# Shifting early work of a gated linear attention and squared-ReLU kernel from GpSimd to ScalarE and VectorE, with a new order of the whole program

## The chip, the cores and the metric

The kernel runs on 1 core of one Trainium2 chip. Times are device microseconds (us) of one launch. The time before is the median of three runs, 177.12 us (176.09, 177.12 and 177.60). One further run was profiled; its trace is what the text reads. Engines are named as in the profile: PE is TensorE, ACT is ScalarE, DVE is VectorE, POOL is GpSimd, SP is SyncE, which only issues transfers here.

## The reference

```python
# q, k, v, alpha: (4, 8, 768, 48) float32; w_in (384, 2048), w_out (2048, 384)
state = zeros((B, H, D, D))
for t in range(S):
    state = alpha[:, :, t, :, None] * state + einsum('bhd,bhe->bhde', k[:, :, t], v[:, :, t])
    y[:, :, t] = einsum('bhd,bhde->bhe', q[:, :, t], state)
x = y.transpose(0, 2, 1, 3).reshape(B * S, H * D)      # 3072 tokens x 384
h = maximum(x @ w_in, 0)
out = (h * h) @ w_out
```

A recurrence with a decay for each channel runs over 768 steps for each batch and head; its output, tokens by 384 features, goes through two matrix products with a squared ReLU between them.

## The kernel before

**Tiles.** The recurrence is computed in chunks of 128 tokens. Two chunks make a *pair* (256 tokens); 3 pairs make a batch element, and G = 12 pairs the whole, numbered g = 0 to 11. Every pair goes through the same stages:

- *loads* (L591): four transfers of 384 KB, in the order alpha, k, q, v, into the float32 buffer RAW (4 buffers).
- *decay* (L621; for pairs 0 and 1 in two halves X of four heads, decay_half, L664): ACT takes the logarithm of alpha (tile lab), PE sums it over the chunk with a triangular matrix, ACT takes exponentials (asb, and the decay over the whole chunk, acp), DVE multiplies q and k by them into bf16 (qks). In values (L612) v is cast to bf16 (vbf): on POOL for pairs 0 and 1 (L616), on ACT for the others (L619).
- *turned* (turned_half, L727, for pairs 0 and 1; turned, L701; turned_dma, L718, from pair 4 on): qks is transposed, by PE and an eviction into qkt, or by a transfer.
- *scores* (L759): PE multiplies k with q inside the chunk into four PSUM tiles of 128x512; DVE multiplies each by a triangular mask and writes bf16 (pm, L780).
- *carry* (L788): PE forms k^T v for each of the two chunks; DVE adds the old state (ust, L817) and POOL multiplies by the decay into the bf16 state (sbf, L819). The first chunk of a batch element has no old state: DVE makes it in one step (L814).
- *mixed* (L826; mixed_back, L897, from pair 4 on): PE sums pm times vbf (the 48 or 64 matmuls that need pm) and state times q (the matmuls of "before", two groups; the second must wait until the first has drained). For pairs 0 to 3 the result comes out transposed, and ACT evicts it chunk by chunk into xt, the transposed input of the MoE part (L879). For the others ACT evicts it into yb and a transfer transposes it into xt.
- *up* (L953): 8 steps u for each pair, 6 matmuls each: 256 hidden features, evicted by ACT with a ReLU (rr, 4 buffers, L973), squared by DVE (gt, L975). It needs both chunks of xt and the piece of win that holds its columns.
- *down* (L989): for each chunk tt four steps p of 4 matmuls each, from gt and wout into a PSUM tile, which ACT evicts and a transfer stores.

In the text "up/0/4" is step 4 of up for pair 0, "down/0/1/3" step 3 of chunk 1 of pair 0, "qks1" the tile qks of pair 1, and so on.

**Order.** Nobody writes the order by hand. Every operation is added to a Program with an engine, an assumed cost, a due time `at` and the tiles that it reads and writes; a list scheduler (Program.order, L147) then runs through assumed time and writes down one instruction list for each engine. At run time each engine executes its list strictly in order and waits by semaphores for what its next instruction needs. The due times come from TABLE (L16), one row for each pair, an offset for each stage. PSUM has eight banks: psG0 to psG3, psO0, psO1, psH0, psH1. POOLS (L30) says from which set the stages of pairs 0 and 1 take their bank; a bank is taken again only when its reader is done. The steps up use psH0 and psH1 in turn; WIDE (L37) counts the first steps that may also use psO0, which the steps down need. Where the scheduler finds PE idle early, it inserts matmuls on a tile of zeros ("warm", L982).

**Weights.** w_in and w_out come in nine pieces on POOL's queue, and the transfer casts them to bf16: win0, win2 (192 KB each), win4, win8, win12 (384 KB each), wout0, wout4, wout8, wout12 (384 KB each). PARTS (L38) makes two runs of them: the first six behind the landing of pair 1's alpha, then the last three. QUEUED (L40) puts the four loads of pair 2 on POOL's queue too, between the two runs. OPENS (L39) holds the loads of pair 3, on SP's queue, until wout8 has landed.

Of the kernel before, what the change touches and what calls it, by code (L numbers as in the profile page):

```python
# [5 lines left out]
ALU = mybir.AluOpType  # L6
AF = mybir.ActivationFunctionType
# [9 lines left out]
    dict(decay0=-101.63878, decay1=-64.79031, turned0=-73.57009, turned1=-62.54519, scores0=-30.02735, scores1=-46.13048, carry=-24.00248, mixed=-12.61483, up=3.82089, down=9.97184, scale00=37.96521, scale01=12.07767, scale10=-55.27694, scale11=66.26176, ends=3.96969, values=3.22532, loads=-198.59615),  # L17
    dict(decay0=-62.3532, decay1=-43.34947, turned0=-42.30728, turned1=-37.91382, scores0=-25.93696, scores1=-11.6373, carry=-24.1783, mixed=3.23949, up=7.51554, down=6.63429, scale00=34.30537, scale01=-58.35352, scale10=17.21724, scale11=40.27209, ends=44.67154, values=2.77668, loads=-199.72423),
    dict(decay=-3.52293, turned=6.45487, scores0=6.82966, scores1=6.65956, carry=-0.27539, mixed=10.50945, up=12.79282, down=3.90935, loads=-64.41188),
    dict(decay=7.24503, turned=8.97861, scores0=9.08238, scores1=9.71941, carry=9.32967, mixed=10.63684, up=15.57323, down=2.06012, loads=-61.40619),  # L20
    dict(decay=7.93117, turned=8.88166, scores0=11.15836, scores1=10.85679, carry=9.32967, mixed=11.76255, up=15.22484, down=2.29842, loads=-62.88919),
    dict(decay=8.06004, turned=10.03837, scores0=11.3686, scores1=10.90735, carry=10.59388, mixed=11.41181, up=16.11414, down=1.46618, loads=5.03271),
    dict(decay=7.68334, turned=10.80342, scores0=11.5973, scores1=11.84935, carry=10.99201, mixed=14.31953, up=16.37508, down=1.46618, loads=5.21441),
    dict(decay=11.20522, turned=12.7234, scores0=13.91124, scores1=13.85916, carry=12.42083, mixed=14.21671, up=16.27226, down=1.75528, loads=11.16392),
    dict(decay=11.49025, turned=11.82737, scores0=13.75226, scores1=14.7438, carry=12.85879, mixed=15.63875, up=17.67473, down=1.71467, loads=9.89433),
    dict(decay=11.5844, turned=11.68949, scores0=14.67671, scores1=14.63718, carry=14.26836, mixed=15.50289, up=17.56635, down=1.71467, loads=9.53939),
    dict(decay=10.86409, turned=12.68953, scores0=16.09372, scores1=14.63718, carry=14.3971, mixed=11.80752, up=17.60364, down=1.71467, loads=10.75129, masks=-31.23894),
    dict(decay=10.86409, turned=12.68953, scores0=15.58331, scores1=14.80708, carry=14.3971, mixed=15.0505, up=17.60364, down=1.71467, loads=10.84157),
# [8 lines left out]
WIDE = 0  # L37
PARTS = ((1, 3, 6), (2, -1, 3))  # L38
OPENS = {3: 7}  # L39
QUEUED = (2,)  # L40
# [385 lines left out]
def bass_gla_recurrent__then__act_relu_squared_kernel(  # L426
# [164 lines left out]
    def loads(g, at):  # L591
        b, t0, r = g // NW, (g % NW) * TW, g % NRAW
        for j, src in ((3, alpha), (0, k), (1, q), (2, v)):
# [5 lines left out]
            if g in QUEUED:  # L599
# [127 lines left out]
    def turned_half(g, X, at):  # L727
# [6 lines left out]
        for z in range(2):  # L734
# [17 lines left out]
            if X == 0:  # L752
                add("ACT", lambda act, dst=dst, src=src: act.activation(dst, src, AF.Copy), 480 * len(names) - 50,
                    at + 0.02 * z + 0.01, reads=[key], writes=[key] + names)
            else:
                add("DVE", lambda dve, dst=dst, src=src: dve.tensor_copy(dst, src), 280 * len(names) + 45,
                    at + 0.02 * z + 0.01, reads=[key], writes=[key] + names)

    def scores(g, at, js=range(NP), late=0.0):  # L759
# [19 lines left out]
        for n, ((i, X), (ps, key)) in enumerate(banks.items()):  # L779
            add("DVE", lambda dve, i=i, X=X, ps=ps: dve.tensor_tensor(  # L780
# [7 lines left out]
    def carry(g, at, spots=None):  # L788
# [17 lines left out]
        for c in chunks:  # L806
# [9 lines left out]
            else:  # L816
                add("DVE", lambda dve, u=u, was=was, pv=pv: dve.tensor_tensor(UST[u][:], pv, was, ALU.add),  # L817
                    270, at + 0.05 * c, reads=[key, ("sbf", old)], writes=[key, ("ust", u)])
                add("POOL", lambda e, u=u, to=to, ac=ac: e.tensor_tensor(to, UST[u][:], ac, ALU.mult),  # L819
                    600, at + 0.05 * c, reads=[("ust", u), ("acp", c_, 0), ("acp", c_, 1)], writes=[("sbf", new)], port=True)  # L820
# [5 lines left out]
    def mixed(g, at, spots=None, between=None):  # L826
# [50 lines left out]
        for c in range(2):  # L877
            ps, key = banks[c]
            add("ACT", lambda act, c=c, ps=ps: act.activation(  # L879
                XT[:, 2 * (g % NX) + c].rearrange("f k (p i) -> f k i p", i=2),  # L880
                ps[:, 0:HD].rearrange("f (k i p) -> f k i p", k=KT, i=2), AF.Copy),
                    435, at + 0.02 * c + 0.01, reads=[key], writes=[key, ("xt", g % NX, c)])
# [145 lines left out]
    def stage(at, fn, *name):  # L1028
        place[name] = at
        stages.append((at, fn, name))  # L1030
# [3 lines left out]
    for g in range(G):  # L1034
        o = TABLE[g]
        stage(2 * g + o["loads"], lambda at, g=g: loads(g, at), "loads", g)
# [69 lines left out]
    for run, (r, j, n) in enumerate(PARTS):  # L1106
        first = pieces[sum(p[2] for p in PARTS[:run])][0]
        ahead(("weights", run), [("weights", run + 1), ("up", 0) if first == "in" else ("down", 0)])
        ahead(("loads", r), [("weights", run)])
    for g in QUEUED:  # L1110
        ahead(("weights", g - 2), [("loads", g)])
# [64 lines left out]
```

## Time and profile before

| what | us |
|---|---|
| median of three runs | 177.12 |
| the runs | 176.09 to 177.60 |
| the profiled execution, own time | 177.66 |
| its span, first to last instruction | 175.9 |
| PE busy in the span | 168.3 |
| DVE busy | 120.3 |
| ACT busy | 116.8 |
| POOL busy | 38.5 |

The granted PE clock is full throughout. The profiled execution's own time is 1.76 us longer than its span. A row of the timeline reads: start in us, busy us, engine, line, operation, written tile <- read tile, shape, count, and in brackets the idle time of the engine just before and what ended it. "psG<-vbf,qks" on PE is carry, "psG<-pm,vbf" and "psG<-qkt,sbf" are mixed, "psG<-qkt" is scores, "psG<-lab,hinc" decay, "<-ident,qks" the transposes, "psH<-xt,win" up and "psO<-wout,gt" down.

### The profile page before, as it was taken

The numbers are of one execution on the slowest core, as the hardware profiler recorded it, in microseconds if no ns is written. First come the engines' busy times: TensorE is split into PE (matmuls) and PEld (weight loads), VectorE is DVE, ScalarE is ACT, GpSimd is POOL, SyncE is SP. The second block draws the span as 40 slices with busy tenths as digits, with TensorE's granted clock in tenths as the row PEclk, the third lists the DMA queues.
The fourth block names the chain that finished last, engine by engine and source line by source line (L and its number), as shares of the span: only waits on it lengthen the run. The fifth ranks groups of instructions, "written<-read, shape, count | busy, mean of one in ns | idle before, by whom it ended". The sixth has DMA issues, their size and how long they took to land.

```text
span 175.9 us, 5997 instructions
## 1 busy us (share of the span) xinstructions
PE 168.3 (96%) x2609; PEld 123.8 (70%) x2609; DVE 120.3 (68%) x253; ACT 116.8 (66%) x233; POOL 38.5 (22%) x68
## 2 busy tenths in 40 slices
PE   7899598999999999999999999999999999999994
PEld 7556466766778677786777777776777777777773
DVE  7887844986899899888737939877885551232220
ACT  3884458666889677489868697767675545656641
POOL 4099820100012001010222131212330302220120
PEclk9999999999999999999999999999999999999999
DMA  5999999899996994999999989999491133212222
GB/s 146 324 294 173 203 338 221 140 276 246 318 321 100 307 304 101 148 315 201 324 201 319 238 159 296 195 321 173 100 182 32 22 71 60 56 22 48 45 45 91
DMA packets 76314, 32.89 MB, mean 187 GB/s; under 512 B 69632, under 2 KB 75456, under 8 KB 76288
## 3 DMA queue, kind: packets, MB, share of 16 engines
q1 hardware_dynamic: 70384, 25.04, 61.4%
q0 software_dynamic: 5904, 7.47, 20.7%
q8 instruction: 20, 0.33, 0.8%
q14 instruction: 6, 0.05, 0.1%
HBM read 25.17 MB, written 4.72 MB: 170 GB/s over the span
## 4 chain that ended last, share of the span: by engine, by line
PE 85%; DMA 9%; POOL 2%; ACT 1%; DVE 1%; issue 1%
PE psO L996 34%; PE psH L963 33%; DMA win<-in_moe_w_in_dram 6%; DMA xt<-yb 3%; PE psG L770 3%; PE psO L982 2%; PE psG L920 2%; POOL win L574 2%; PE psG L799 2%; PE psG L838 2%; PE psO L1015 2%; PE psG L910 1%; PE psG L710 1%; PE psG L637 1%; DVE qks L691 1%; ACT asb L688 1%
## 5 line engine op out<-in xcount | busy, mean ns | idle before, releaser
L973 ACT ACTIVATE rr<-psH 128x512 bf16<-128x512 f32 x96 | 58.2, 611 | 37.6 <-PE psH L963 36.5
L963 PE MATMUL psH<-xt,win 128*128 128x256 bf16 x576 | 75.8, 273 | 2.5 <-DMA win<-in_moe_w_in_dram 2.1
L996 PE MATMUL psO<-wout,gt 128*128 128x384 bf16 x368 | 71.5, 326 | 0.7 <-ACT xt L879 0.7
L975 DVE TENSOR_TENSOR gt<-rr 128x512 bf16<-128x512 bf16 x96 | 41.4, 439 | 38.4 <-ACT rr L973 37.9
L963 PEld LDWEIGHTS psH<-xt,win 128*128 128x128 bf16 x576 | 54.0, 98 | 16.1 <-ACT rr L973 3.1
L996 PEld LDWEIGHTS psO<-wout,gt 128*128 128x128 bf16 x368 | 35.0, 98 | 17.3 <-ACT xt L879 0.9
L949 POOL DMA_DIRECT2D out_dram<-osb x28 | 15.1, 544 | 71.3 <-ACT osb L1003 71.0
L780 DVE TENSOR_TENSOR pm<-psG,mask 128x512 bf16<-128x512 f32 x45 | 28.7, 682 | 1.8 <-PE psG L770 0.6
L819 POOL TENSOR_TENSOR sbf<-ust,acp 128x192 bf16<-128x192 f32 x16 | 9.3, 580 | 52.4 <-DVE ust L817 52.3
L658 DVE TENSOR_TENSOR qks<-raw,asb 128x768 bf16<-128x768 f32 x20 | 18.3, 951 | 3.2 <-ACT asb L647 3.2
L1003 ACT ACTIVATE osb<-psO 128x384 f32<-128x384 f32 x23 | 11.4, 494 | 3.7 <-PE psO L996 3.2
L647 ACT ACTIVATE asb<-psG 128x384 bf16<-128x384 f32 x20 | 9.8, 492 | 2.9 <-PE psG L639 2.6
L627 DVE TENSOR_TENSOR raw<-raw 128x384 f32<-128x384 f32 x20 | 11.0, 564 | 0.1
L770 PEld LDWEIGHTS psG<-qkt 64*64 64x64 bf16 x360 | 6.0, 106 | 4.3 <-issue 2.7
L770 PE MATMUL psG<-qkt 64*64 64x128 bf16 x360 | 8.7, 220 | 0.1
L619 ACT ACTIVATE vbf<-raw 128x768 bf16<-128x768 f32 x10 | 8.5, 853 | 0.2 <-DMA raw<-in_v_dram 0.2
L936 ACT ACTIVATE yb<-psG 128x384 bf16<-128x384 f32 x14 | 6.4, 490 | 2.5 <-PE psG L910 1.8
L982 PE MATMUL psO<-warm 128*128 128x128 bf16 (+1 forms) x39 | 7.0, 343 | 1.1 <-DVE warm L518 1.1
L817 DVE TENSOR_TENSOR ust<-psG,sbf 128x192 f32<-128x192 f32 x15 | 5.3, 353 | 2.5 <-PE psG L799 1.4
L627 DVE TENSOR_TENSOR raw<-raw,ro 128x384 f32<-128x384 f32 x10 | 6.1, 612 | 0.2 <-DMA raw<-in_q_dram 0.2
L643 ACT ACTIVATE ro<-raw 128x384 f32<-128x384 f32 x10 | 5.2, 518 | 0.4 <-DMA raw<-in_alpha_dram 0.4
L633 ACT ACTIVATE lab<-raw 128x384 bf16<-128x384 f32 x10 | 5.2, 524 | 0.2 <-DVE raw L627 0.2
(98 smaller groups left out, 131.0 us busy)
## 6 DMA issues: line engine op xcount, KB each, us to landing
raw<-in_alpha_dram SPq DMA_DIRECT2D x11, 384.0 KB, 4.7
raw<-in_k_dram SPq DMA_DIRECT2D x11, 384.0 KB, 4.8
raw<-in_q_dram SPq DMA_DIRECT2D x11, 384.0 KB, 4.8
raw<-in_v_dram SPq DMA_DIRECT2D x11, 384.0 KB, 5.6
out_dram<-osb POOLq DMA_DIRECT2D x28, 96.0 KB, 3.3
out_dram<-osb SPq DMA_DIRECT2D x9, 192.0 KB, 4.3
wout<-in_moe_w_out_dram POOLq DMA_DIRECT2D x4, 384.0 KB, 14.3
win<-in_moe_w_in_dram POOLq DMA_DIRECT2D x3, 384.0 KB, 9.5
```

The lines of the kernel that those rows point to most:

```text
L627: add("DVE", lambda e: e.tensor_tensor(dst, a0, a1, ALU.mult), 470, at_, reads=reads, writes=writes, port=True)
L647: add("ACT", lambda act, z=z: act.activation(ASB[a][:, z, 0, :], ps[:, 0:HD], AF.Exp, scale=2.0 * z - 1.0), 372, at + 0.04 + 0.02 * z, rea ...
L658: add("DVE", lambda dve, z=z, decays=decays: dve.tensor_tensor(QKS[x][:, z, :, :, 0:D], both(r, z), decays, ALU.mult), 870, at + 0.05 + 0. ...
L770: last = pe.matmul(banks[i, j // 2][0][64 * c:64 * c + 64, col:col + 128].rearrange("p (a b) -> p a b", a=2), QKT[t][64 * i:64 * i + 64, 0 ...
L780: add("DVE", lambda dve, i=i, X=X, ps=ps: dve.tensor_tensor(PMB[m][:, i, 2 * X:2 * X + 2].rearrange("p j n s -> p j (n s)"), ps[:].rearran ...
L949: add(by, lambda e, dst=dst, ps=ps: e.dma_start(dst, OSB[o][ps, :]), 600, at + 0.01 * i, reads=[("osb", o)], dma=("own" if by == "POOL" el ...
L963: last = pe.matmul(ps[:, f * TW:(f + 1) * TW].rearrange("p (c t) -> p c t", c=2), WIN[:, kt, fj * 128:(fj + 1) * 128], XT[:, 2 * (g % NX): ...
L973: add("ACT", lambda act: act.activation(ro, ri, AF.Relu), 480, at, reads=[key], writes=[key, ("rr", r)])
L975: add("DVE", lambda dve: dve.tensor_tensor(gt[:, 2 * u:2 * u + 2, :], rr, rr, ALU.mult), 340, at, reads=[("rr", r)], writes=[("gt", g % NG ...
L982: last = pe.matmul(psO[1][:, 0:128 * wide].rearrange("p (a b) -> p a b", a=wide), WARM[:], bass.AP(tensor=WARM, offset=0, ap=[[128, 128], ...
L996: last = pe.matmul(ps[:, 0:DM], GT[g % NGT][:, fj, tt * 128:(tt + 1) * 128], WOUT[:, fj, :], start=(fj == 0), stop=(fj == FT - 1))
L1003: add("ACT", lambda act: act.activation(OSB[o][:], ps[:, 0:DM], AF.Copy), 372, at, reads=[key], writes=[key, ("osb", o)])
```

## The change

For pairs 0 and 1 four kinds of operation change their engine, by new constants:

- CASTS: the cast of v goes from POOL to ACT (the code of the other pairs, L619).
- STATES: the three products ust times decay (the second chunk of pair 0, both of pair 1) go from POOL to DVE.
- XTS: the second of the two evictions of xt goes from ACT to DVE.
- COPIED: one of the four mask products of each pair is made in two steps: ACT copies the PSUM tile into an rr buffer in bf16, and DVE multiplies that by the mask. That is tile 1 (second score bank of the first half) for pair 0 and tile 2 for pair 1.
- TURNS: the eviction of the second transposed half of pair 1 goes from DVE to ACT.

Beside that the whole order is new: all numbers of TABLE, POOLS and WEIGHTS, and WIDE is 10 instead of 0, so that all steps up of pair 0 and the first two of pair 1 rotate over psH0, psH1 and psO0, and the first step down comes behind them. The loads of pairs 0 and 1 get due times of their own for alpha, for k and q, and for v.

What the two built programs show, engine by engine:

- SP issues the loads of pairs 0 and 1 in the same order as before. Further on, pair 5's loads stand ahead of the first two stores of output instead of behind the first.
- POOL: the two casts and three of the state products are gone; the nine pieces of weights and the loads of pair 2 stand in the same order as before.
- PE has the same work (96 steps up, 100 down, 33 groups of mixed, 22 of scores, 14 of decay, 12 of transposes, 11 of carry) and the same count of changes between matmul forms behind down/0/1/3. In the first 40 us its order differs, as follows.

PE before, from the second decay on: scores/0 (first half), transposes of pair 1's first half, carry/0, mixed/0 (48), transposes of the second half between the two groups of mixed/0, scores/1 (first), up/0/0, up/0/1, scores/1 (second), up/0/2 to up/0/6, carry/1, mixed/1 (48), up/0/7, down/0/1/0, the two groups of mixed/1, down/0/0/0, up/1/0, and so on.

PE after: scores/0 (both halves, ahead of pair 1's decay), transposes of the first half, mixed/0 (48), transposes of the second half, carry/0, first group of mixed/0, carry/1, second group of mixed/0, scores/1 (first), up/0/1, up/0/0, scores/1 (second), up/0/2, up/0/3, mixed/1 (48) and its first group, up/0/4, its second group, up/0/5, up/0/6, up/0/7, up/1/0 to up/1/3, down/0/0/0, up/1/4, up/1/5, decay/2, down/0/1/0, up/1/6, up/1/7, down/0/0/1, carry/2, transposes of pair 2, down/0/0/2, down/0/1/1, down/0/1/2, scores/2, down/0/0/3, down/0/1/3.

```diff
 TABLE = [
-    dict(decay0=-101.63878, decay1=-64.79031, turned0=-73.57009, turned1=-62.54519, scores0=-30.02735, scores1=-46.13048, carry=-24.00248, mixed=-12.61483, up=3.82089, ...
+    dict(decay0=-97.00571, decay1=-78.81219, turned0=-80.03886, turned1=-50.01967, scores0=-30.48193, scores1=-47.68772, carry=-27.42287, mixed=-10.34508, up=13.54943, ...
...
-POOLS = [dict(decay=0, turned=2, scores=2, carry=1, mixed=2), dict(decay=2, turned=2, scores=1, carry=0, mixed=1)]
-WEIGHTS = (-75.69063, -62.43345)
+POOLS = [dict(decay=1, turned=2, scores=2, carry=1, mixed=2), dict(decay=0, turned=1, scores=1, carry=1, mixed=0)]
+WEIGHTS = (-75.27555, -73.28278)
...
-WIDE = 0
+WIDE = 10
...
-QUEUED = (2,)
+QUEUED = ((2, None, 'loads', 0),)
+CASTS = ('ACT', 'ACT')
+STATES = ('DVE', 'DVE')
+XTS = ('DVE', 'DVE')
+COPIED = ((1,), (2,))
+TURNS = ('DVE', 'ACT')
...
     def values(g, at):
...
-        if g < FIRST:
+        if g < FIRST and CASTS[g] == "POOL":
...
     def turned_half(g, X, at):
...
-            if X == 0:
+            if X == 0 or TURNS[g] == "ACT":
...
     def scores(g, at, js=range(NP), late=0.0):
...
+            if g < FIRST and 2 * X + i in COPIED[g]:
+                r = copied[0] % NRR
+                copied[0] += 1
+                add("ACT", lambda act, ps=ps, r=r: act.activation(RR[r][:], ps[:], AF.Copy), 480, at + late + 0.01 * n,
+                    reads=[key], writes=[key, ("rr", r)])
+                add("DVE", lambda dve, i=i, X=X, r=r: dve.tensor_tensor(
+                    PMB[m][:, i, 2 * X:2 * X + 2].rearrange("p j n s -> p j (n s)"),
+                    RR[r][:].rearrange("p (j s) -> p j s", j=2), mask, ALU.mult),
+                    340, at + late + 0.01 * n, reads=[("rr", r), "mask"], writes=[("pm", m, i, X)], port=True)
+                continue
...
     def carry(g, at, spots=None):
...
-                add("POOL", lambda e, u=u, to=to, ac=ac: e.tensor_tensor(to, UST[u][:], ac, ALU.mult),
-                    600, at + 0.05 * c, reads=[("ust", u), ("acp", c_, 0), ("acp", c_, 1)], writes=[("sbf", new)], port=True)
+                by = STATES[g] if g < FIRST else "POOL"
+                add(by, lambda e, u=u, to=to, ac=ac: e.tensor_tensor(to, UST[u][:], ac, ALU.mult),
+                    600 if by == "POOL" else 270, at + 0.05 * c, reads=[("ust", u), ("acp", c_, 0), ("acp", c_, 1)], writes=[("sbf", new)], port=True)
...
     def mixed(g, at, spots=None, between=None):
...
+            if g < FIRST and c == 1 and XTS[g] == "DVE":
+                add("DVE", lambda dve, dst=dst, src=src: dve.tensor_copy(dst, src), 470, at + 0.02 * c + 0.01,
+                    reads=[key], writes=[key, ("xt", g % NX, c)])
+                continue
```

More of the change, by code (lines that the diff above doesn't have):

```diff
@@ L1108, in bass_gla_recurrent__then__act_relu_squared_kernel @@
         ahead(("weights", run), [("weights", run + 1), ("up", 0) if first == "in" else ("down", 0)])
[L1109 to L1111 removed]
+        if r >= FIRST:
+            ahead(("loads", r), [("weights", run)])
+    for g in range(FIRST):
+        ahead(("loads", g), [("pair", g)])
+        ahead(("pair", g), [("last", g)])
+        ahead(("last", g), [("decay", g)])
+        for run, (r, j, n) in enumerate(PARTS):
+            if r == g and j >= 0:
+                ahead((("pair", g) if j < 2 else ("last", g) if j == 2 else ("loads", g)), [("weights", run)])
+    for g, j, name, run in QUEUED:
+        ahead(("weights", run), [(name, g)])
+        if run + 1 < len(PARTS):
+            ahead((name, g), [("weights", run + 1)])
     for g, x in OPENS.items():
```

45 lines of the change are left out of this document (25 added, 20 removed).

## The prediction

> **What bounds the kernel now.** First the page's parts 1 and 2: which engine fills the span, and where it does not.
>
> ```profile
> span 175.9 us, 5997 instructions
> PE 168.3 (96%) x2609; PEld 123.8 (70%) x2609; DVE 120.3 (68%) x253; ACT 116.8 (66%) x233; POOL 38.5 (22%) x68
> PE   7899598999999999999999999999999999999994
> PEclk9999999999999999999999999999999999999999
> ```
>
> PE is the bound at full clock. Its only thin slices are the first six (4.4 us each, to 26 us) and the last one. The windows view gives the same by stage (PE first, DMA share second to last):
>
> ```profile
> 20.00:24.00 4.00, 2.26 (x22) 1.66 (x26) 2.54 (x4) 1.68 (x3) 1.32 (x2) 1.00 1.22 272
> 28.00:32.00 4.00, 3.96 (x39) 3.08 (x40) 1.99 (x5) 4.00 (x11) 0.00 (x0) 1.00 1.30 202
> 40.00:50.00 10.00, 10.00 (x192) 7.33 (x190) 7.62 (x15) 7.22 (x16) 0.00 (x0) 1.00 1.06 289
> ```
>
> From 28 us on PE has no gap to speak of, so whatever the change does to DVE, ACT or POOL there is worth nothing unless PE has to wait. A gain can only come from the head: useful matmuls done before 28 us that now run later. What PE waited for, from the waits of PE:
>
> ```profile
> PE psH L963 <- DMA win<-in_moe_w_in_dram: 2.1, 3, 1.5
> PE psO L996 <- ACT xt L879: 0.7, 1, 0.7
> ```
>
> That is 2.8 us, 2.1 for pieces of win and 0.7 for the xt of pair 1. PE's timeline shows where:
>
> ```profile
> 12.45 0.44 PE L799 MATMUL psG<-vbf,qks 64*64 64x48 bf16 x32
> 16.29 1.48 PE L963 MATMUL psH<-xt,win 128*128 128x256 bf16 x12
> 21.40 1.47 PE L963 MATMUL psH<-xt,win 128*128 128x256 bf16 x12 [1.55 <-DMA win<-in_moe_w_in_dram]
> 23.21 0.82 PE L963 MATMUL psH<-xt,win 128*128 128x256 bf16 x6 [0.34 <-DMA win<-in_moe_w_in_dram]
> 25.00 0.83 PE L963 MATMUL psH<-xt,win 128*128 128x256 bf16 x6
> 25.67 0.81 PE L996 MATMUL psO<-wout,gt 128*128 128x384 bf16 x4
> 27.92 0.82 PE L996 MATMUL psO<-wout,gt 128*128 128x384 bf16 x4 [0.71 <-ACT xt L879]
> 28.58 0.82 PE L963 MATMUL psH<-xt,win 128*128 128x256 bf16 x6
> 37.63 2.76 PE L996 MATMUL psO<-wout,gt 128*128 128x384 bf16 x16
> 40.32 0.86 PE L838 MATMUL psG<-pm,vbf 64*64 64x128 bf16 x48
> ```
>
> At 21.40 PE stood 1.55 us for win8 while carry and mixed of pair 1 were still to do: they ran at 24 to 27 us, behind the steps up that wait for weights. Why they were not ready is in POOL's timeline:
>
> ```profile
> 8.36 0.82 POOL L616 CAST vbf<-raw 128x768 bf16<-128x768 f32 x1 [4.80 <-DVE qks L691]
> 9.34 4.01 POOL L574 DMA_DIRECT2D win<-in_moe_w_in_dram  x5 [0.16 <-issue]
> 19.85 0.90 POOL L616 CAST vbf<-raw 128x768 bf16<-128x768 f32 x1
> 24.97 0.61 POOL L819 TENSOR_TENSOR sbf<-ust,acp 128x192 bf16<-128x192 f32 x1 [3.56 <-DVE ust L817]
> 26.05 0.51 POOL L819 TENSOR_TENSOR sbf<-ust,acp 128x192 bf16<-128x192 f32 x1 [0.47 <-DVE ust L817]
> ```
>
> The cast of pair 1's v stood on POOL behind all issues of weights and of pair 2 (19.85); carry/1 needs it; then two state products on POOL, ending 25.58 and 26.56, stand before the last groups of mixed/1.
>
> **The change, part by part.** The anchor is the state "up/0/7, mixed/1 and xt of pair 1 done, up/1/0 about to start". Before, that is 28.58 with two steps down (0.65 each) done too. I follow the changed order to the same state. Rows of ACT and of DVE:
>
> ```profile
> 9.07 0.94 ACT L670 ACTIVATE lab<-raw 128x384 bf16<-128x384 f32 x2 [0.35 <-DMA raw<-in_alpha_dram]
> 10.19 1.92 ACT L688 ACTIVATE asb<-psG 128x384 bf16<-128x384 f32 x4 [0.18 <-PE psG L676]
> 12.56 1.02 ACT L753 ACTIVATE qkt<-psG 128x1024 bf16<-128x1024 bf16 x1 [0.25 <-PE psG L742]
> 14.23 0.61 ACT L879 ACTIVATE xt<-psH 128x384 bf16<-128x384 f32 x1 [0.65 <-PE psH L838]
> 31.75 0.86 ACT L619 ACTIVATE vbf<-raw 128x768 bf16<-128x768 f32 x1
> 35.19 1.25 ACT L973 ACTIVATE rr<-psH 128x512 bf16<-128x512 f32 x2 [1.60 <-PE psH L963]
> 10.94 1.12 DVE L691 TENSOR_TENSOR qks<-raw,asb 128x384 bf16<-128x384 f32 x2
> 13.65 0.35 DVE L814 TENSOR_TENSOR sbf<-psG,acp 128x192 bf16<-128x192 f32 x1
> 17.02 0.68 DVE L780 TENSOR_TENSOR pm<-psO,mask 128x512 bf16<-128x512 f32 x1
> 17.79 0.42 DVE L975 TENSOR_TENSOR gt<-rr 128x512 bf16<-128x512 bf16 x1
> ```
>
> *Casts of v.* On ACT a cast is 0.86 us (31.75). Pair 0's stands between the evictions of qkt (done about 8.6) and pair 1's logarithm, which therefore starts at 9.35 instead of 9.07: 0.3 us on the path. On POOL the issue of weights no longer waits for a cast, only for pair 1's alpha (9.07): 0.27 us earlier at most, and 0 at least, since the transfers share engines that are already full (DMA share 1.22 at 20 to 24 us). I take 0.1 for the landings.
>
> *Mask in two steps.* ACT pays 0.6 (a copy of 128x512, half of 1.25), DVE 0.42 instead of 0.68. Pair 0's copy stands on ACT between the logarithms and the exponentials of pair 1, so these run 10.7 to 12.65 instead of 10.19 to 12.11: with the cast 0.5 us later.
>
> *State products on DVE.* 0.35 each (the nearest row, L814, has the same shape) instead of 0.61 and 0.51, and no hand-over between engines. If DVE takes longer from SBUF than from PSUM, POOL's 0.61 is the high end. Nothing excludes less: from 192 to 512 elements a product grows from 0.35 to 0.68, 1 ns an element, so 0.2 without any fixed part is the low end. I take 0.35, the row of the same shape.
>
> *Second xt eviction on DVE.* No row; between 0.35 (192 elements) and 0.68 (512), so 0.53 for 384, against 0.61 on ACT. The ends, 0.18 us either way, go into the range. The second transposed half of pair 1 costs ACT 1.02 more.
>
> *The chain.* ACT: exponentials to 12.65; first transposed half of pair 1 at 13.25 (qks ready 12.75, and 0.5 as before: 12.06 to 12.56) to 14.3; first xt of pair 0 14.2 to 14.8, as before (14.23); cast of v1 14.65 to 15.5; second transposed half 15.4 to 16.4. DVE: third mask 10.94 to 11.6, two qks to 12.75, bf16 mask to 13.1, two qks to 14.05. PE: mixed/0 (48) 13.15 to 14.0, the transposes to 14.4, carry/0 14.45 (before 12.45); DVE makes the three state steps 15.0 to 15.9; carry/1 waits for the cast, 15.55 to 16.0; second group of mixed/0 to 16.35; DVE's xt 16.4 to 16.95; the first step up at 17.0. **That is 0.7 us later than before (16.29); so far the change loses.**
>
> Then steps up at 0.655 each (1.31 for two: 28.58 and its followers): up/0/1 and up/0/0 to 18.35, scores/1 (second) to 18.7, up/0/2 and up/0/3 to 20.1. Meanwhile DVE does masks and states; its list ends with the bf16 mask at 20.25. mixed/1 (48) 20.3 to 21.1, its first group to 21.4, **in the time in which PE stood for win8**; up/0/4 21.45 to 22.1 (win8 landed before 21.4), second group to 22.4, up/0/5 to 23.1, up/0/6 behind win12 (23.2 before, 23.1 now) to 23.8, up/0/7 to 24.5. DVE's xt of pair 1 is done at 23.05, so up/1/0 follows at once: the anchor state at 24.5, without the two steps down.
>
> From there to the end of down/0/1/3 PE needed 40.24 - 28.58 = 11.66 us before (37.63 and 2.6 us of 16 matmuls); with the two steps down, 1.30, it is 12.96, so 37.46 now. **Gain 40.24 - 37.46 = 2.78 us.** As a check: the waits of the head that go are 2.1 + 0.7 = 2.8. Behind that point both orders hold the same matmuls and as many changes of form, so the rest takes 175.9 - 40.24 us in both, if PE does not wait.
>
> Does it? PE now reaches the weights sooner. Landings, from the transfers by window (us from issue to landing) and SP's own queue:
>
> ```profile
> raw<-in_v_dram SPq DMA_DIRECT2D x1, 384.0 KB, 4.9
> win<-in_moe_w_in_dram POOLq DMA_DIRECT2D x1, 384.0 KB, 10.5
> wout<-in_moe_w_out_dram POOLq DMA_DIRECT2D x1, 384.0 KB, 13.7
> 33.28 0.37 SPq L604 DMA_DIRECT2D raw<-in_alpha_dram  x1
> ```
>
> The v of pair 1, issued at 7.79, landed at 12.7, 2 us before its cast. The last piece of win landed at 23.1; wout4, issued at 17.63, at 31.3; wout8 just before 33.28. Behind 24.5 come eight steps up, two down and decay/2 (0.25), so the changed order asks for wout4 at 24.5 + 5.2 + 1.3 + 0.3 = 31.3, and for wout8 behind carry/2 and the transposes of pair 2 at about 33.3: no slack, no wait. ACT was busy for all 4.00 us at 28 to 32 us with PE at 3.96: nearly a second bound, now in the same stretch. I cost both at nothing; what hides them is just enough, and without that cover up to 1 us comes back, the high end. The first step down now needs psO0 free from up/1/1, which is evicted a step before; that costs nothing while ACT keeps up. On SP, pair 5's loads pass two stores; a store that waits holds nobody, as there are eight buffers for the output. Later, before had one wait of PE on a transfer in all:
>
> ```profile
> 134.84 0.82 PE L963 MATMUL psH<-xt,win 128*128 128x256 bf16 x6 [0.25 <-DMA xt<-yb]
> ```
>
> There mixed/8 ended 8 us of PE work ahead of the step up that needs it or the next; counted by the same durations along the new list of PE, pairs 7 to 11 have 10 to 15 us, so 0.25 more can go, and pairs 4 to 6 have about as much room as before.
>
> *The pages.* The Trainium skill, "SBUF — State Buffer", section "Who interferes with whom", says that a VectorE instruction with two SBUF inputs contends with a GpSimd instruction that reads SBUF. The trace agrees:
>
> ```profile
> 19.38 2.31 DVE L975 TENSOR_TENSOR gt<-rr 128x512 bf16<-128x512 bf16 x3
> ```
>
> Three squares took 0.77 each in place of 0.42 while POOL cast v (19.85); by that rule about 1 us of DVE time comes back in the head. It is off PE's path there, so my sum does not use it.
>
> **The rivals.**
>
> *A. As above.* Span 175.9 - 2.78 = 173.1, own time 174.9. The profiled execution (177.66) lies 0.54 above the median shown, so against the median 177.12 - 2.75 = 174.4. Own range: 173.3 (the wait at 134.84 gone, weights 0.27 earlier, states at 0.2) to 175.3 (1 us lost at wout4, wout8 or ACT).
>
> *B. PE runs into transfers that it outran.* The order is ahead of the data: 31.3 asked against 31.3 landed, and pair 3's loads still start only when wout8 has landed (33.28). Each 0.5 us that a landing slips is a wait at wout4, wout8 or at pair 3's transposes, and up to 2 us of the gain go. For it speaks the DMA share of 1.2 to 1.3; against it, that PE has steps of pair 1 to do in between. Time 177.1 - 1.1 = 176.0.
>
> *C. Slower: the cast on ACT in front of carry/1.* PE is in order: carry/1 stands ahead of the second group of mixed/0, and so of every step up. If v1's cast ends late (v1 landing later because weights start earlier, or ACT's queue of 8 to 15 us slipping), all steps up slip with it. To cancel the gain the cast must end 2.8 us later, at 18.3 instead of 15.5; that needs v1 to land at 17.4 rather than 12.7, or ACT, DVE and PE handing over 0.2 us slower at each of some 14 steps from 9 to 17 us. With 4.5 us of delay the time is 177.1 + 1.7 = 178.8. The slack of 2 us on v1 speaks against it; that every step of this stretch is a hand-over speaks for it.
>
> *D. Nothing changes:* the time of the head is set by win12's landing at 23.1 whatever stands before it, and the work taken out of the gap comes back as waits for ACT. Time 177.1 - 0.1 = 177.0.
>
> **How the numbers follow.** A 0.62, B 0.20, C 0.12, D 0.06. The predicted time is A's, 174.4. The range goes from A's low end, 173.3, through B and D to 177.1, leaving out C and little else. About 1%, 1.8 us (175.3 to 178.9), is what a measurement of this kernel can tell from no change. Faster by over 1%: A and a fifth of B, 0.66. Within: the rest of B, D and some of C, 0.24. Slower: 0.10.
>
> **What would show it.** Right: in the changed trace the first step up starts later than 16.29, near 17.0; mixed/1 of PE stands at 20 to 22 us; no wait of over 0.5 us for win; up/1/0 starts near 24.5; down/0/1/3 ends near 37.5; POOL computes nothing between 4 and 30 us. Wrong: up/1/0 later than 26 (C), or PE waits of over 1 us in all between 25 and 60 us on transfers of wout, raw or on ACT (B), or a wait for the transposes behind 60 us.

## The result and the profile after

The changed kernel takes **174.18 us** (median of six runs, 173.92 to 175.52), the kernel before in the same rounds 177.03 (176.09 to 177.60). The ratio is 0.9859, with a 95% interval of 0.9817 to 0.9902. Forecast were 174.4 us and a range of 173.3 to 177.1. The profiled execution took 174.21 us, its span is 172.5.

The page's parts 1 and 2 of the changed kernel:

```profile
span 172.5 us, 6016 instructions
PE 167.6 (97%) x2611; PEld 123.9 (72%) x2611; DVE 119.4 (69%) x257; ACT 116.9 (68%) x236; POOL 36.4 (21%) x63
PE   7889999999999999999999999999999999999994
```

The thin slices of PE behind the third have gone. The waits of PE:

```profile
PE psO L1004 <- DVE warm L523: 1.1, 1, 1.1
PE psH L747 <- DVE qks L696: 0.4, 1, 0.4
PE psG L856 <- issue: 0.3, 1, 0.3
PE psG L747 <- DVE qks L696: 0.3, 1, 0.3
```

Neither win nor xt is in the list any more; what is left lies before 21 us. PE's timeline:

```profile
14.36 0.44 PE L816 MATMUL psG<-vbf,qks 64*64 64x48 bf16 x32
16.74 0.83 PE L985 MATMUL psH<-xt,win 128*128 128x256 bf16 x6
20.02 0.64 PE L856 MATMUL psG<-pm,vbf 64*64 64x128 bf16 x32
20.98 0.42 PE L856 MATMUL psG<-pm,vbf 64*64 64x128 bf16 x16 [0.32 <-issue]
21.50 0.83 PE L985 MATMUL psH<-xt,win 128*128 128x256 bf16 x6
23.88 1.47 PE L985 MATMUL psH<-xt,win 128*128 128x256 bf16 x12
31.34 0.81 PE L1018 MATMUL psO<-wout,gt 128*128 128x384 bf16 x4
35.97 2.88 PE L1018 MATMUL psO<-wout,gt 128*128 128x384 bf16 x16
```

The reader is to see mixed/1 at 20.02, where before PE stood for win8. The row at 23.88 holds up/0/7 and up/1/0, so up/1/0 starts at about 24.54 with no gap. The last row holds four steps, of which down/0/1/3 is the second: it ends near 37.4, and before that was 40.24. At 20.98 a pause of PE in the midst of mixed/1 ends, for which the profile names no wait ("issue"). From its start to up/0/4 mixed/1 takes 1.48 us here, 0.96 in a run without a pause that is shown below, so the pause costs about 0.5. A few rows of ACT, of DVE and of POOL:

```profile
14.48 0.83 ACT L624 ACTIVATE vbf<-raw 128x768 bf16<-128x768 f32 x1
```
```profile
15.65 0.36 DVE L837 TENSOR_TENSOR sbf<-ust,acp 128x192 bf16<-128x192 f32 x1
16.09 0.59 DVE L900 CAST xt<-psH 128x384 bf16<-128x384 f32 x1
19.55 0.41 DVE L792 TENSOR_TENSOR pm<-rr,mask 128x512 bf16<-128x512 bf16 x1
19.89 1.66 DVE L997 TENSOR_TENSOR gt<-rr 128x512 bf16<-128x512 bf16 x4
```
```profile
9.50 4.00 POOL L579 DMA_DIRECT2D win<-in_moe_w_in_dram  x5 [5.95 <-DMA raw<-in_alpha_dram]
```

v1's cast ends at 15.31, and nothing stands on POOL between the issues. The last mask of pair 1 ends at 19.96, 0.06 us before mixed/1 starts: DVE's list now sets that start.

### The profile page after: what moved, and what is told of

It is laid out like the page before. It is cut to its first block, busy times and chain, and to the rows that moved or that the text cites. A ratio compares the mean times of both kernels' runs of the same rounds, so it can differ in the third digit from the quotient of the medians.

```text
span 172.5 us, 6016 instructions
## 1 busy us (share of the span) xinstructions
PE 167.6 (97%) x2611; PEld 123.9 (72%) x2611; DVE 119.4 (69%) x257; ACT 116.9 (68%) x236; POOL 36.4 (21%) x63
## 4 chain that ended last, share of the span: by engine, by line
PE 95%; DVE 2%; issue 1%; ACT 0%
PE psH L985 36%; PE psO L1018 36%; PE psG L777 4%; PE psO L1004 3%; PE psG L856 2%; PE psG L942 2%; PE psG L816 2%; PE psO L1037 2%; PE psG L932 2%; PE psO L985 2%; DVE qks L696 2%; PE psG L642 1%; PE psG L715 1%; PE psG L681 1%; PE psH L856 1%
## 5 line engine op out<-in xcount | busy, mean ns | idle before, releaser
L995 ACT ACTIVATE rr<-psH 128x512 bf16<-128x512 f32 x92 | 55.3, 612 | 22.6 <-PE psH L985 20.6
L985 PE MATMUL psH<-xt,win 128*128 128x256 bf16 x552 | 70.5, 273 | 0.0
L1018 PE MATMUL psO<-wout,gt 128*128 128x384 bf16 x368 | 70.0, 326 | 0.0
L985 PEld LDWEIGHTS psH<-xt,win 128*128 128x128 bf16 x552 | 52.7, 98 | 11.6 <-DVE xt L900 0.2
L997 DVE TENSOR_TENSOR gt<-rr 128x512 bf16<-128x512 bf16 x96 | 40.3, 434 | 29.6 <-ACT rr L995 29.3
L1018 PEld LDWEIGHTS psO<-wout,gt 128*128 128x128 bf16 x368 | 34.3, 98 | 17.8 <-ACT osb L1025 0.3
L797 DVE TENSOR_TENSOR pm<-psG,mask 128x512 bf16<-128x512 f32 x44 | 27.9, 682 | 3.7 <-PE psG L777 2.9
L624 ACT ACTIVATE vbf<-raw 128x768 bf16<-128x768 f32 x12 | 10.1, 842 | 0.0
L632 DVE TENSOR_TENSOR raw<-raw,ro 128x384 f32<-128x384 f32 x10 | 5.5, 551 | 0.8 <-DMA raw<-in_q_dram 0.5
L654 ACT ACTIVATE ro<-ro 128x384 f32<-128x384 f32 x10 | 5.2, 524 | 0.1
```

The lines of the kernel that those rows point to most:

```text
L624: add("ACT", lambda act: act.activation(dst, src, AF.Copy), 740, at, reads=raw(r, 2), writes=[("vbf", vb)])
L632: add("DVE", lambda e: e.tensor_tensor(dst, a0, a1, ALU.mult), 470, at_, reads=reads, writes=writes, port=True)
L797: add("DVE", lambda dve, i=i, X=X, ps=ps: dve.tensor_tensor(PMB[m][:, i, 2 * X:2 * X + 2].rearrange("p j n s -> p j (n s)"), ps[:].rearran ...
L985: last = pe.matmul(ps[:, f * TW:(f + 1) * TW].rearrange("p (c t) -> p c t", c=2), WIN[:, kt, fj * 128:(fj + 1) * 128], XT[:, 2 * (g % NX): ...
L995: add("ACT", lambda act: act.activation(ro, ri, AF.Relu), 480, at, reads=[key], writes=[key, ("rr", r)])
L997: add("DVE", lambda dve: dve.tensor_tensor(gt[:, 2 * u:2 * u + 2, :], rr, rr, ALU.mult), 340, at, reads=[("rr", r)], writes=[("gt", g % NG ...
```

## The experiments

In seven kernels the changed kernel's own order was kept: its finished lists were taken and single operations were moved from one engine's list to another's, nothing else. "Row of up/0/7" is the start of the PE row that is at 23.88 in the changed kernel; both columns of rows are from the one profiled execution of each kernel. The ratio is to the kernel before on the same chip.

| kernel | median us (runs) | ratio, 95% interval | first step up | row of up/0/7 |
|---|---|---|---|---|
| changed | 174.18 (6) | 0.9859, 0.9817 to 0.9902 | 16.74 | 23.88 |
| casts on POOL, v1's behind the issues | 181.90 (4) | 1.0290, 1.0258 to 1.0321 | 22.93 | |
| casts on POOL, v1's between the issues | 174.28 (4) | 0.9868, 0.9840 to 0.9895 | 17.26 | 23.88 |
| states on POOL, between the issues | 174.62 (4) | 0.9866, 0.9833 to 0.9898 | 16.67 | 23.65 |
| second xt on ACT | 174.64 (4) | 0.9891, 0.9864 to 0.9918 | 17.05 | 24.19 |
| masks in one step | 174.44 (4) | 0.9879, 0.9853 to 0.9905 | 16.78 | 23.75 |
| transposed half on DVE | 174.32 (4) | 0.9873, 0.9838 to 0.9909 | 16.82 | 23.52 |
| all five moves undone | 175.06 (5) | 0.9914, 0.9891 to 0.9936 | 17.93 | 25.14 |
| moves with the old numbers | 176.85 (10) | 1.0022, 0.9995 to 1.0049 | 18.89 | |
| two copies before v1's cast | 175.60 (10) | 0.9939, 0.9902 to 0.9977 | 19.06 | 27.11 |
| four copies before v1's cast | 178.44 (10) | 1.0049, 1.0007 to 1.0090 | 19.53 | 26.16 |
| weights issued 1 us later | 175.66 (10) | 0.9926, 0.9892 to 0.9960 | 16.69 | 23.92 |

One thing has to be known for reading the last column. Ten of these kernels have the changed kernel's list on PE. Of their profiles only one, that with the second xt on ACT, has a pause in mixed/1 as long as the changed kernel's (20.28 to 21.82, 1.54 us up to up/0/4); the others need 0.96 to 1.10 us there, for 1.48. So up to 0.5 us of any delay ahead of mixed/1 is made up at this place, and a row of up/0/7 that is no later does not show by itself that a move costs nothing. How many of the executions that were not profiled have the pause is not known.

**The place of the casts.** Theory: what held carry/1 and mixed/1 back was the place of v1's cast behind all issues on POOL. Rival D: the landing of win12 sets the head, whatever stands before it. Two kernels put both casts back on POOL; `move` takes an operation to another engine's list, behind a named one or at its planned time.

```diff
+    issue = [o for o in pr.programs["POOL"] if o.dma is not None][:13]
+    pr.move(kept["cast", 0][0], "POOL", [o for o in pr.programs["POOL"] if o.start < issue[0].start][-1], ...)
+    pr.move(kept["cast", 1][0], "POOL", issue[-1], ...)
```

> The changed kernel with both casts of v back on POOL at the places they had before: pair 0's ahead of the weights, pair 1's behind all issues of weights and of pair 2's loads; every other list is kept as it is. Theory (the gain is pair 1's carry and mixed done before win8, and the cast's place in POOL's queue kept them from it): the cast ends at about 21.0 instead of 15.3, carry/1 and with it every step up slips by 5.5 us; PE regains some of it since it is ahead of the weights by 0.6 us only, so +4.5 us, 178.7, slower than before. Rival (the weights' landing sets the head, rival D): no more than 0.5 us is lost, 174.7.

Measured: 181.90 us, ratio 1.029. D is out. Its loss, 7.7 us, is larger than the theory had; its wait and windows of PE (granted clock third from the end) say why:

```profile
PE psO L836 <- POOL vbf L642: 5.3, 1, 5.3
```
```profile
16.00:20.00 4.00, 0.00 (x0) 0.00 (x0) 0.02 (x1) 0.00 (x0) 4.00 (x7) 0.65 1.22 197
20.00:24.00 4.00, 3.08 (x61) 1.99 (x62) 1.77 (x4) 0.00 (x0) 0.87 (x2) 0.50 1.23 265
24.00:28.00 4.00, 4.00 (x36) 2.67 (x34) 2.59 (x7) 1.56 (x3) 0.00 (x0) 0.57 1.07 303
```

PE waited 5.3 us for the cast (15.65 to 20.93). The granted clock fell 1.5 us into that wait, at 17.16, and stayed at half until 27.40, so for 6.5 us behind it: the page has PE busy for 170.7 us, against 167.6. So 5.3 of waiting and 3.1 of slower work, less what was free.

```diff
+    for g in range(2):
+        pr.move(kept["cast", g][0], "POOL", None, kept["cast", g][1])
```

> As the run before, but pair 1's cast stands on POOL between the loads of pair 2, where its due time puts it, about 15 us. Theory: it is the place in the queue that counts, not the engine; the cast ends about 15.5 to 16.5, carry/1 slips by 0.2 to 1 us, and the issues behind it by 0.9 us, so wout4 to wout12 land 0.5 to 0.9 later against a slack of 0.5: 174.2 to 175.5. Rival (POOL as such is what costs): as slow as the run before, 178 or more.

Measured: 174.28 us. On the same engine, but among the loads of pair 2:

```profile
15.06 0.84 POOL L642 CAST vbf<-raw 128x768 bf16<-128x768 f32 x1
```
```profile
17.26 0.83 PE L1005 MATMUL psH<-xt,win 128*128 128x256 bf16 x6
20.54 0.86 PE L876 MATMUL psG<-pm,vbf 64*64 64x128 bf16 x48
21.50 0.83 PE L1005 MATMUL psH<-xt,win 128*128 128x256 bf16 x6
```

The time is that of the changed kernel within the noise, and 7.6 us less than behind the issues: the place in the queue counted, not the engine. That the rows agree to 0.01 us from up/0/4 on, though the first step up is 0.52 later, is a coincidence: mixed/1 starts 0.52 later as well, and does not pause in this run.

**The other moves, one by one.**

```diff
+    for g, c in ((0, 1), (1, 0), (1, 1)):
+        pr.move(kept["state", g, c], "POOL")
```

> The changed kernel with the three state products back on POOL, each where its planned start puts it among the issues on POOL's queue; everything else is kept. Theory: each product takes 0.58 instead of 0.35 plus a hand-over each way, and waits up to 0.9 us for the issue in front of it; up/0/0 needs the bank that the second one frees, mixed/1 the third: 1 to 2 us later in the head, 175.2 to 176.2. Rival (the states are off PE's path): under 0.3 us, 174.4.

Measured: 174.62 us, by the ratios 0.1 us more than the changed kernel, so the rival's "under 0.3". In the head mixed/1 starts 0.20 later (20.22); up/0/4 is 0.22 earlier (21.28 for 21.50) only because the long pause is not there. Its profiled execution took 177.38, for another reason, which the run's waits show:

```profile
PE psH L1005 <- DMA xt<-yb: 1.7, 1, 1.7
```

That is a transposing transfer that came late at 72 us, once. Behind it the granted clock fell to half for 3.41 us (two steps up at 74.47 took 2.74 us for 1.47), so this one late transfer was paid for twice. It is the kind of wait that the prediction had named as a risk "behind 60 us"; the changed kernel's profile has none.

```diff
+    for g in range(2):
+        pr.move(kept["xt", g][0], "ACT", None, kept["xt", g][1])
```

> Only the second eviction of xt of pairs 0 and 1 back on ACT, order kept. ACT idles where pair 0's falls (16.1 us) and takes 0.61 for 0.59; pair 1's falls into a stretch where ACT has 0.3 us to spare in 4. Theory: 174.2 (174.0 to 174.6), the first step up within 0.1 of 16.74. Rival (this move frees the ACT that PE would wait for): 174.8 or more, with waits of PE for rr or xt of 0.5 us between 22 and 32 us.

Measured: 174.64 us; 0.3 us later all along from the first step up, so the row of up/0/7 shows no further loss; no wait for rr or xt. Of the 0.3 us, 0.27 are there before the first xt (mixed/0 starts at 13.29, for 13.02). Between the two expectations, and not told apart from the changed kernel by the intervals.

```diff
+    for g in range(2):
+        copy, fn, two = kept["mask", g]
+        pr.programs["ACT"].remove(copy)
...
+        two.fn = fn
...
```

> Only the masks in one step again, order kept: ACT does two copies of 0.6 less, DVE pays 0.26 more for each of two masks. The prediction put ACT's copy of pair 0 on the path with 0.2 us, the mask of pair 1 at the end of the list that opens mixed/1. Theory: the exponentials of pair 1 run 0.5 earlier, the first step up 0.0 to 0.4 earlier than 16.74; mixed/1 is not earlier than 20.0, as DVE's last mask is 0.26 later; time 174.2 (173.9 to 174.5). Rival (the copy unloads DVE, which sets mixed/1): mixed/1 at 20.4 or later and up/1/0 0.3 later, time 174.5 to 174.8.

Measured: 174.44 us, inside the theory's range and 0.06 below the rival's, so the time does not tell them apart; the first step up is 0.04 later, where the theory had it up to 0.4 earlier. The mask of pair 1 is later, and PE waits for it; up/0/4 is not (21.37), as the long pause is missing here:

```profile
20.33 0.94 PE L876 MATMUL psG<-pm,vbf 64*64 64x128 bf16 x48 [0.30 <-DVE pm L810]
```

```diff
+    pr.move(kept["turn", 1, 1][0], "DVE", None, kept["turn", 1, 1][1])
```

> Only the eviction of pair 1's second transposed half back on DVE, order kept. DVE pays some 0.6 to 0.8 us at about 15 us, just where it makes the three states and the xt that open the first step up. Theory: the first step up 0.4 to 0.8 later (17.1 to 17.5), mixed/1 0.3 to 0.5 later, up/1/0 at most 0.3 later, as 0.5 of such a delay was free when the cast stood on POOL: time 174.2 to 174.6. Rival (the delay is paid in full): 174.8 to 175.0.

Measured: 174.32 us; the first step up is only 0.08 later, less than expected, as is mixed/1 (20.10), and up/0/7 is 0.36 earlier, again for want of the pause. No single move of the last three is worth anything that these runs resolve.

**All five moves undone, the new order kept:** the edits on the casts (between the issues), the states, xt, the masks and the transposed half, together.

> All five engine moves undone, every engine's order of the rest as in the changed kernel; the cast of v1 and the three state products stand on POOL between the issues, where their inputs are ready, not behind them. Theory (the order is the gain and the engines are hardly any of it; casts and states undone by themselves cost 0.1 and 0.4 us at most): 174.2 to 174.9, up/1/0 between 24.2 and 25.2. Rival (the moves cover for one another, and only together do they make the order possible): 175.5 to 177.0, up/1/0 behind 25.8.

Measured: 175.06 us, ratio 0.9914: the order alone keeps about 1.5 us of the gain of 2.5 (0.0086 and 0.0141 of 177 us), the engines together are worth the other 1.0. This split is rough, as the two intervals just touch. Both theories missed: the time lies between them, and up/1/0, at about 25.8, on the rival's bound. The profile is of the slowest of the five runs (176.73), which lost 1.17 us more on a transposing transfer at 94 us; what follows on the head is from this one run. From 23.88 to 25.14 are 1.26 us; mixed/1 starts 1.78 later (21.80), and does not pause. 0.36 is there from the start (the first issue of win is at 9.86, for 9.50). Most of the rest is in DVE's list:

```profile
17.90 0.36 DVE L854 TENSOR_TENSOR ust<-psO,sbf 128x192 f32<-128x192 f32 x1 [0.63 <-POOL sbf L857]
20.19 0.36 DVE L854 TENSOR_TENSOR ust<-psG,sbf 128x192 f32<-128x192 f32 x1 [0.75 <-POOL sbf L857]
21.07 0.68 DVE L810 TENSOR_TENSOR pm<-psG,mask 128x512 bf16<-128x512 f32 x1
```

DVE waits twice for POOL's states and pays 0.68 for the last mask, which ends at 21.75 instead of 19.96. Each undoing alone delays mixed/1 by 0.08 to 0.52 us, no more than the pause costs in the changed kernel's profile; together they delay it by more.

**The moves alone, with the numbers of before** in TABLE, POOLS, WEIGHTS and WIDE.

```diff
-POOLS = [dict(decay=1, turned=2, ...
+POOLS = [dict(decay=0, turned=2, ...
-WIDE = 10
+WIDE = 0
```

> The operations on their new engines, but planned with the numbers of before (TABLE, POOLS, WEIGHTS, WIDE 0; the loads of pairs 0 and 1 in the order of before). The scheduler by itself then puts mixed of pair 1 ahead of up/0/2, and down/0/0/0, which needs wout0 (landed 24.3 to 25.1), between up/0/5 and up/0/6. Theory: the engines bring most of the gain, a wait for wout0 of 1 to 2 us takes part of it back: 175.5. Rival (the new numbers bring the gain): 177.

Measured: 176.85 us, ratio 1.0022: nothing gained, as the rival had it; the wait for wout0 that the theory counted on is not there. The profile is of the slowest of the ten runs (178.32), so a part of what it shows may be missing in the others. PE and DVE of this kernel:

```profile
18.89 1.48 PE L985 MATMUL psH<-xt,win 128*128 128x256 bf16 x12
22.54 0.21 PE L856 MATMUL psG<-pm,vbf 64*64 64x128 bf16 x1 [1.47 <-issue]
```
```profile
16.78 0.69 DVE L797 TENSOR_TENSOR pm<-psG,mask 128x512 bf16<-128x512 f32 x1
17.38 0.68 DVE L797 TENSOR_TENSOR pm<-psO,mask 128x512 bf16<-128x512 f32 x1
18.25 0.58 DVE L900 CAST xt<-psH 128x384 bf16<-128x384 f32 x1
```

The old numbers put two masks and a state ahead of the xt that opens the first step up, on the engine to which it was moved: 18.89 instead of 16.74. Which of the new numbers matter most was not tried. And PE stood for 1.47 us in the midst of mixed/1's 48 matmuls, where no semaphore is waited for. One more kernel asks what that is: 40 instead of 28 matmuls on the tile of zeros at PE's start, the order as it was.

```diff
-WARMUP = (28, 1)
+WARMUP = (40, 1)
```

> The kernel with the moves and the old numbers, with 40 instead of 28 matmuls on the tile of zeros at the start of PE, all else in the same order. In its run PE stood 1.47 us in the midst of the 48 matmuls of mixed/1, behind the 38th, with nothing that it waited for. Theory (PE's instructions come by transfers, a block at a time, and a block came late): 24 more instructions move the place 12 matmuls ahead, behind the 26th of the 48, with 1 to 2 us again. Rival (the place belongs to the operation or its data): behind the 38th again, or nothing there.

Measured, in its one run (177.23 us):

```profile
22.02 0.21 PE L856 MATMUL psG<-pm,vbf 64*64 64x128 bf16 x1 [0.42 <-issue]
```

That matmul is the 28th of the 48; in the kernel without the addition it is the 40th. The place moved by exactly the 12 matmuls that were added; the pause is shorter than the 1 to 2 us expected. (The expectation counted 38 and 26 before the pause; the rows have 39 and 27.) The pause belongs to a place in PE's stream of instructions, not to the data. Counted in the traces, 705 instructions of PE (matmuls, weight loads and those on semaphores) stand ahead of it in both kernels, and also ahead of the pause in the changed kernel and in the one with the second xt on ACT, which share another list on PE.

**A later cast.** How much slack has rival C's chain? Copies of v1 into a tile that nobody reads stand on ACT ahead of its cast, two in the one kernel and four in the other.

```diff
-            add("ACT", lambda act: act.activation(dst, src, AF.Copy), ...
+            add("ACT", lambda act: [act.activation(to, src, AF.Copy) for to in idle + [dst]][-1], ...
```

> The changed kernel with two more copies of v1 (into a tile that nobody reads) on ACT just ahead of the cast of v1: the cast ends about 1.5 to 1.7 us later, all other orders as they were. Theory (rival C's chain with a slack of 0.5 us, as the cast on POOL showed; the rest is paid in full): the first step up near 18.3, time 175.3 (174.9 to 175.7). Rival one (the time is set by win8 and win12 anyway, D): 174.2 to 174.6. Rival two (PE's granted clock falls after the wait): 176 or more, with less than 1.00 granted between 16 and 24 us.

> The same with four more copies: the cast ends about 3.0 to 3.4 us later. The prediction said that 2.8 us would cancel the gain. Theory (0.5 free, the rest in full): 176.9 (176.5 to 177.3), so that it takes about 3.3 us and not 2.8. Rival one (D): below 175. Rival two (the clock falls, as behind the wait of 5.3 us for the cast behind all issues): 178 or more.

Measured: 175.60 and 178.44 us. The times of each fall into two groups, 175.04 to 175.77 (six runs) and 176.27 to 177.56 (four); 176.49 to 176.90 (three) and 178.04 to 179.48 (seven). The mean granted clock is on record for each run: with four copies it is 1.00 in the lower three and 0.98 to 0.99 in all of the upper seven, with two copies 0.99 in two of the upper four (176.54 and 177.56) and 1.00 in the other eight. The two profiles happen to be one of each kind, first two copies, then four:

```profile
17.71 0.21 PE L819 MATMUL psO<-vbf,qks 64*64 64x48 bf16 x1 [1.20 <-ACT vbf L626]
19.06 1.46 PE L988 MATMUL psH<-xt,win 128*128 128x256 bf16 x6
```
```profile
16.00:18.00 2.00, 0.80 (x41) 0.49 (x42) 0.81 (x3) 2.00 (x4) 2.00 (x3) 1.00 1.21 191
20.00:22.00 2.00, 2.00 (x21) 1.19 (x23) 1.08 (x3) 0.16 (x1) 0.58 (x1) 0.50 1.27 201
```
```profile
18.23 0.21 PE L819 MATMUL psO<-vbf,qks 64*64 64x48 bf16 x1 [2.66 <-ACT vbf L626]
19.53 0.83 PE L988 MATMUL psH<-xt,win 128*128 128x256 bf16 x6
```
```profile
20.00:22.00 2.00, 2.00 (x33) 1.56 (x31) 1.97 (x5) 0.95 (x2) 0.00 (x0) 1.00 1.29 206
```

In the second profile (own time 176.49) the clock stayed at 1.00; the first step up is 2.79 late and up/0/7 2.28 late (26.16). The 0.51 between them is the pause, which is missing here (mixed/1 takes 0.96 us); the rest was paid in full: 174.2 + 2.3 = 176.5, as measured. So what the theory took for slack is the pause, and without it rival C's chain has none to be seen. In the first profile (177.56) the clock fell to 0.50, and a step up of 6 matmuls took 1.46 us for 0.83. So the theory's time is that of the lower group of each kernel, and the second rival, the clock, gives the upper group with four copies; with two copies it gives two of the four slower runs, and what slowed the other two is open.

**Later weights.** Two fills of an unused tile on POOL, ahead of the first issue of win.

```diff
...
-                fn = lambda g, ...: g.dma_start(WIN[:, :, w], win_src[:, :, w])
+                fn = lambda g, ..., late=2 * (x == 0): [g.memset(IDLE[:, y], 0.0) for y in range(late)] + [
+                    g.dma_start(WIN[:, :, w], win_src[:, :, w])]
```

> The changed kernel with two fills of an unused 128x768 float32 tile on POOL ahead of the first issue of win, so that all nine pieces of weights and pair 2's loads are issued later by their length (unknown, taken as 1 to 1.5 us together). Measured slack so far: win8 landed 0.6 us ahead of up/0/4, wout4 0.5 ahead of its step. Theory (B: landings follow the issue, and the slack is 0.5 to 0.6): PE waits for win8 and the like, time up by the delay less 0.6, 174.6 to 175.1. Rival (landings are set by the transfer engines, which are full, and move by less than half of the delay): 174.0 to 174.4 and no wait for win or wout over 0.3 us.

Measured: 175.66 us (174.75 to 176.77); the profiled execution 175.0. POOL, then PE:

```profile
10.49 4.01 POOL L582 DMA_DIRECT2D win<-in_moe_w_in_dram  x5
```
```profile
19.03 0.83 PE L988 MATMUL psH<-xt,win 128*128 128x256 bf16 x6 [0.51 <-DMA win<-in_moe_w_in_dram]
31.72 0.82 PE L1021 MATMUL psO<-wout,gt 128*128 128x384 bf16 x4 [0.18 <-DMA wout<-in_moe_w_out_dram]
```

With the issues 0.99 us later, a wait for win4 comes back and one for wout4 is new, 0.7 us in all, and the profiled run is 0.8 us above the changed kernel's. The loss of the medians, about 1.2 us by the ratios (0.0067 of 177), is more than the theory's 0.4 to 0.9, but the intervals overlap, and where more than 0.7 goes is not shown. The rival is out. B's mechanism is real, and its margin is small.

## Why the prediction was right

*A's anchor and sum.* Predicted: up/1/0 at 24.5, down/0/1/3 ending at 37.46, a gain of 2.78. The trace: 24.54, about 37.4, so 2.8. The mechanism is as told: mixed/1 runs in the time in which PE stood for win8, and the first step up is later than before (16.74 for 16.29; 17.0 was forecast) and yet nothing is lost. The medians give 177.03 - 174.18 = 2.85. That the anchor fits to 0.04 us is in part luck: mixed/1 started 0.28 earlier than forecast (20.02 for 20.3), and a pause of about 0.5 us, of which the prediction knew nothing, took that back.

*Casts.* Right that a late cast of v1 holds mixed/1 and every step up; by itself an early one was not enough, as the moves with the old numbers show. The durations held (0.83 for 0.86). What the prediction put to the engine belongs to the place: between POOL's issues the cast does as well, within the noise.

*Weights.* Taken: issued 0 to 0.27 earlier, landed 0.1 earlier. Measured: issued 0.16 later (9.50) and yet landed earlier. From issue to landing for the v of pair 2 and for wout4, and SP's own issue of pair 3's alpha, which follows wout8:

```profile
raw<-in_v_dram POOLq DMA_DIRECT2D x1, 384.0 KB, 12.1
wout<-in_moe_w_out_dram POOLq DMA_DIRECT2D x1, 384.0 KB, 13.0
```
```profile
32.78 0.37 SPq L609 DMA_DIRECT2D raw<-in_alpha_dram  x1
```

wout4 landed at 17.78 + 13.0 = 30.8, wout8 0.5 us earlier than before. So B's premise, "no slack", was wrong by half a microsecond in the good direction. One profile could not show this: in those of the twelve other kernels the row that stands at 32.78 starts between 32.33 and 33.61. Whether the change did it, or the one profile of before was a late one, is open.

*Mask, states, xt.* Costed as 0.42, 0.35 and 0.53; measured 0.41, 0.36 and 0.59. The gain did not hang on them one by one: states on POOL cost nothing that can be measured as long as they stand between the issues. In the sum the prediction treated the five moves and the order as one; the runs part them roughly into 1.5 us for the order and 1.0 for all the moves. The moves alone gain nothing that can be measured, and no single move loses anything that can be when it is undone at a place where its inputs are ready.

*The rule on two SBUF inputs.* The Trainium skill, "SBUF — State Buffer", section "Who interferes with whom", has a VectorE product of two SBUF tiles contend with GpSimd reads. The trace agrees: with no cast on POOL the four squares at 19.89 took 0.415 each, for 0.77 before.

*The wait at 134.84* is gone, as the prediction allowed. That and 0.4 us more, spread in PE's busy time (168.3 to 167.6) and not located, make the spans differ by 3.4; the profiled execution of before was itself 0.6 above its median.

*Rival C* was priced at the right point and with too little behind it: 2.87 us of delay (the cast ended at 18.18 for 15.31) brought the time to 176.5 to 176.9 in the three runs with the clock at 1.00, but to 178.0 to 179.5 in the other seven.

## What to carry to other kernels

Look for the place where PE waits for data that cannot come sooner, and ask which work that is due later could stand there; then ask what keeps that work from being ready. It is often one small operation behind a row of issues on the same queue, and another place on that queue can be as good as another engine. Moves and order have to be planned together: here each without the other brought part of the gain or none.

## What the runs showed of the hardware

*PE can pause for its own instructions.* 1.47 and 0.42 us in the kernels with the old numbers, 0.32 us in the changed one and 0.37 in the one with the second xt on ACT, each time behind 705 recorded instructions of PE; each pause was at 20.7 to 22.5 us, when the transfer engines were full (DMA share 1.22 to 1.25). The Trainium skill, "Runtime: NRT & Kernel Launch", section "Instruction fetch mechanics", says that instructions come in blocks of 256 by a transfer queue of their own, which is mostly hidden. The trace agrees on the stream: it has 20 transfers of 16 KB on a queue of instructions, and in each of the four runs the last one ahead of the pause ended 1.3 to 1.6 us before PE went on (18.76 to 19.72 in the changed kernel, where PE went on at 20.98). Here the pause was not hidden. That the full transfer engines made the block late is argued, not shown; these four transfers themselves took 0.89 to 0.97 us, no longer than others of their queue later on (0.88 to 1.63 in the changed kernel).

*A short wait of PE can cost twice.* The granted clock fell to 0.50 behind a wait of 1.20 us (two copies), behind one of 1.66 us (the late transfer at 72 us), and 1.5 us into the wait of 5.3 us. It stayed there for 3.41, 3.41 and 10.24 us, so for one or three times 3.41. Behind a wait of 2.66 us it did not fall in the profiled run, but in seven of the ten runs of that kernel the mean clock was below 1.00. The Trainium skill, "TensorE: Matmul & The Clock Gate", section "Part 1: The HAM clock gate", puts the fall behind an idle window of about 3.4 us, whose place runs freely. The steps of 3.41 us agree, and a freely running window fits that runs of one kernel differ. But PE had not been idle for that long before any of the three falls, so the clock falls sooner than that rule says, and the measurement decides. How much work keeps the clock up is not settled: it fell behind 3.41 us with PE busy for 2.21 (15.41 to 18.82, two copies), and held behind 3.41 us with PE busy for 1.86 in the kernel before (19.24 to 22.65).
